# Fused attention and two expert layers on one core: the gate's clamp, log and sum in two column halves, and a start that is dealt out anew

## The chip, the cores and the metric

The kernel runs on one core of a Trainium2 chip, as one program. The metric is the device time of one launch in microseconds (us). Engines are named as in the profile: PE multiplies matrices, PEld is its weight load, DVE works on vectors, ACT evaluates functions, POOL is GpSimd, and SP issues the DMAs.

## The reference

Three blocks follow each other, all in float32. The kernel returns the last one.

```python
# attention with a decay: B, H, S, D = 4, 8, 576, 64
scores = (1/sqrt(D)) * q @ k.T
cum = cumsum(log(clip(f, 1e-4, 1.0)))          # one row of 576 gates for each of 32 heads
scores = where(causal, -1e9, scores + cum[:, None] - cum[None, :])
attn = softmax(scores) @ v                     # to x: 2304 tokens x 512
# first expert layer
x = ((x @ w1) * (x @ w2)) @ w3 @ w_out         # 512 -> 1024 -> 1024 -> 512
# second expert layer, on the normalized x
x = x / sqrt(mean(x*x) + 1e-6) * rms_g
out = silu(x @ w_gate) * (x @ w_val) @ w_out2  # 512 -> 1536 -> 512
```

## The kernel before

All work is listed as operations of a planner (`Plan`). Each has an engine, or a choice of engines, an estimated time, and the keys that it reads and writes. `Plan.order()` works out one order for each engine from these estimates and from due times, and the instructions are issued in that order. The keys serve the planner alone; the waits that the program really holds are put in by the framework, tile by tile. `TE` is the step between the due times of the first eight heads, `WC0` the due time of the first weight product.

**Heads.** Each of the 32 heads has 576 queries in five blocks. PE multiplies queries and keys into the PSUM tile `wide` (block 4) and into two banks (blocks 3 and 0, 2 and 1). DVE adds the mask and takes the row maximum (L439, tiles `PB0` to `PB4` and `nmax`; letters a and b for even and odd heads), ACT takes the exponential with the row sum (L447), PE transposes (L484), ACT and DVE copy the result (`PTf` for the first three heads, L500; `PTh` and `PTl` later), and PE multiplies it with the values into `wide` (L530 and L540). The tile `wide` serves scores and output in turn, so the next use waits until DVE has read it.

**Gates.** The decay comes in as additional rows of the factors: for the first two heads (`NQ`) rows 64 and on of `rq` and `rk` hold the cumulative sum, times 8 and times -8, beside constants. `start()` makes them. The gates of all heads are loaded in one DMA to `fc` (112 rows: the 32 heads twice, then heads 0 and 1 over the partitions that feed those rows), clamped on DVE (L1094), logged on ACT (L1095) and summed along the row by a scan on DVE (L1096) into `cum`. `first_rows` then writes the row block of `rq` on DVE (L1109) and of `rk` on ACT (L1111). The rows 64 to 127 of `rq` and `rk` were cleared before that on DVE (L1084). `cqx` takes the sums for the later heads (L1116, L1117, L260), which go to DRAM and come back head by head.

**Warming.** While PE has nothing to do it multiplies zeros (`zeros`, L1075): 7 products of 448 columns (`WARM`) at the start, and 4 more around the first head's scores. Nobody reads them.

**Weights.** The weights of the first layer arrive packed, and are unpacked (L572, L576 or L578, L582) and split into a high and a low part (L258 or L260, L251) on whichever of ACT, DVE and POOL the planner picks. 192 products (L656) of `w3` and `w_out` fill PE beside the first eight heads. When these heads are done `x_split` makes `xhl`, and the products of the first layer (L693, L718) follow, beside the rest of the heads. The second layer (L905, L986) comes when all heads are done.

Of the kernel before, what the change touches and what calls it, by code (L numbers as in the profile page):

```python
# [14 lines left out]
F32R = mybir.dt.float32r  # L15
U32 = mybir.dt.uint32
AF = mybir.ActivationFunctionType
# [5 lines left out]
P = 128  # L23
# [21 lines left out]
NR = 4  # L45
KH = KF2 // 2
FROWS = 112
WARM = 7
NQ, NP, QD = 2, 3, 6
WIDER = 3  # L50
NST = 3
# [1 line left out]

S0, TE, T1 = 0, 8200, 13400
LT, LP = 5000, 13000

WC0, WCP = 22000, 9000

FD, FR = 25000, 1.8

# [154 lines left out]
def body(ctx, tc, q, k, v, f, w12, w3, wo1, wgv, wo2, g, out):  # L217
# [13 lines left out]
    def t_dve(n, rate=1.04, lock=False):  # L231
        return "DVE", 70 + rate * n, lock

    def t_act(n, fixed=95):
        return "ACT", fixed + 0.833 * n, False
# [91 lines left out]
    cq = cqx[0:NH]  # L327
    cn = X[1].rearrange("p r n -> p (r n)")[0:NH, 0:2 * S].rearrange("p (r n) -> p r n", r=2)

    def load_f():  # L330
        SP.dma_start(out=fc, in_=f)

    def load_g():
        SP.dma_start(out=g_sb, in_=g)
# [107 lines left out]
    def row_exp(h, i, at):  # L442
        p, pr = h % 2, h // 2 % 2
        n, cols = QB[i][1], QEND[i]
        o = PB[p][i][:n, 0:cols]
        to = o if i else PB[p][4][0:n, 512:576]
        act(cols + 225, lambda: A.activation(to, o, AF.Exp, bias=nmax[p][:n, i:i + 1], scale=-1.0, accum_out=rsum[pr][:n, p, (i - 1) % 5:(i - 1) % 5 + 1]),  # L447
            [("nmax", p, i)] + ([] if i else [("PB", p, 4)]), [("PB", p, i), ("rsum", pr, p, i)], at)

    def attn_s(h, at):  # L450
        p = h % 2
# [1 line left out]
        t = t.rearrange("p (c n) -> p c n", c=2)  # L453
        QKh, w = QK, 1
        if h < NQ:
            QKh, w = [("rq", p), ("rk", p, 0), ("nrowq", p), ("nrown", p)], 2
        n1, n2 = st_next(h), st_next(h)
        o4 = [t[:, c, 0:288] for c in range(2)]
        o3, o0 = bank[n1][:, 0:448], bank[n1][0:64, 448:512]
# [14 lines left out]
    def transpose(h, parts, o, key, pt, at):  # L474
# [22 lines left out]
            for j in range(2):  # L497
                dma(147e3, lambda j=j: SP.dma_start(out=rall[j * D:(j + 1) * D, :], in_=r_o[j, 0:S].partition_broadcast(D)), [("rd", h // 2)], [("rall", j)])
        if h < NP:
            plan.op([t_act(n, 55), t_dve(n)], lambda e: (A.copy if e == "ACT" else V.tensor_copy)(PTf()[:, pt:pt + n], o[:, lo:lo + n]), [], [("PTf", pt), key] + ["fc", "one32", "cum"] * (h == 0))  # L500
            return
        act(n, lambda: A.copy(PTh[:, pt:pt + n], o[:, lo:lo + n]), [], [("PTh", pt), key], at, 55)  # L502
        m = n if pt != PT_KB3 else PT_Q0
# [571 lines left out]
        pe(896, lambda: T.matmul(bank[n][:, 0:448], mask[:, 0:P], mask[:, 0:448], start=True, stop=True), ["mask0", *r], [("bank", n)], at, 2)  # L1075

    def start():
        dma(157e3, load_f, w=["fc"], at=-100)
        load_qk(0, -90)
        dma(2e3, load_g, w=["g"], at=50000)  # L1080
        dve(300, lambda: V.memset(mask, 0.0), w=["mask", "mask0"])
        for p in range(2):

            dve(1030, lambda p=p: (V.memset(rq[p][D:P, :], 0.0), V.memset(rk[p][D:P, :], 0.0)), w=[("nrowq", p), ("nrown", p), ("rk", p, 1)])  # L1084

        for i in range(WARM):
            zeros(5, -1000)
        pool(580, make_ones, w=["one32", "cn1"], at=-50)
        pool(1100, make_masks, w=["ident", "mask", "ones"], at=-40)
        pool(2000, make_zeros, w=["zeros"], at=-30)  # L1090
        dve(70, lambda: V.memset(rows_c, 1.0), w=["picks"])
        dve(70, lambda: (V.memset(under, -0.501), V.memset(exp_in, 0.0)), w=["under", "exp"])
        act(1500, lambda: A.activation(rows_c[:, 0:1], rows_c[:, 0:1], AF.Ln), [], ["picks"])
        dve(300, lambda: V.tensor_scalar(out=fc, in0=fc, scalar1=1.0e-4, scalar2=1.0, op0=ALU.max, op1=ALU.min), ["fc"], ["fc"], -100)  # L1094
        act(S, lambda: A.activation(fc, fc, AF.Ln), ["fc"], ["fc"], -100)  # L1095
        dve(S + 650, lambda: V.tensor_tensor_scan(out=cum, data0=one32, data1=fc, initial=0.0, op0=ALU.mult, op1=ALU.add), ["fc", "one32"], ["cum"], -100)  # L1096
        hi, lo = cqx[:, 0, :], cqx[:, 1, :]

        def first_rows(h):
            r = slice(D + 32 * h, D + 32 * h + 4)  # L1100
            e = [ident[r, r.start + i:r.start + i + 1] for i in range(2)]
            c = rows_c[r, :]

            def picks():
                V.tensor_scalar_mul(c[:, 0:1], e[0], 8.0)
                V.tensor_scalar_mul(c[:, 1:2], e[1], -8.0)

            dve(100, picks, ["ident"], ["picks"])
            dve(480, lambda: V.tensor_scalar(out=rq[h][r, :], in0=cum[r], scalar1=c[:, 0:1], scalar2=e[1], op0=ALU.mult, op1=ALU.add),  # L1109
                ["cum", "ident", "picks"], [("nrowq", h)])  # L1110
            act(S, lambda: A.activation(rk[h][r, :], cum[r], AF.Identity, scale=c[:, 1:2], bias=e[0]),  # L1111
                ["cum", "ident", "picks"], [("nrown", h), ("rk", h, 1)], fixed=380)

        for h in range(NQ):
            first_rows(h)
        act(S, lambda: A.activation(hi.bitcast(F32R), cum, AF.Copy, scale=8.0), ["cum"], ["cq0"], -100)  # L1116
        dve(S, lambda: V.scalar_tensor_tensor(out=lo.bitcast(F32R), in0=cum, scalar=8.0, in1=hi, op0=ALU.mult, op1=ALU.subtract), ["cum", "cq0"], ["cq"], -100)  # L1117
        plan.op([("ACT", 1500, False)], lambda e: A.activation(exp_in, exp_in, AF.Exp), ["fc"], ["exp"], 0)
        copy(2 * S, cn, cq, ["cq", "cn1"], ["cn"], -1.0)
        prep(0, -90)  # L1120
        pool(1750, lambda: make_qk_rows(G), w=["rows", "Q2", "K2"])
        dma(150e3, lambda: SP.dma_start(out=cq_d, in_=cq), ["cq"], ["cdq"])
        dma(150e3, lambda: SP.dma_start(out=cn_d, in_=cn), ["cn"], ["cdn"])
        load_v(0, -70)
        prep_v(0, -60)
# [135 lines left out]
```

## Time and profile before

| what | value |
| --- | --- |
| median of 3 runs | 929.91 us (928.27 to 930.31) |
| the profiled execution | 930.35 us |
| its span in the trace | 928.5 us (1.85 us lie around it) |
| PE busy | 915.6 us, 99% of the span |
| PEld busy | 851.1 us, 92% |
| DVE busy | 802.9 us, 86% |
| ACT busy | 541.0 us, 58% |
| POOL busy | 144.4 us, 16% |
| granted TensorE clock | 1.00 |

Busy time is counted from an instruction's start to its end, and the instructions of an engine that overlap count once. The shares are means over a start, a stretch with heads, a stretch with heads and the first layer, and the second layer; the stretches are limited by different engines, so they are read stage by stage.

### The profile page before, as it was taken

Reading aid. Unit: us, or ns where it says so; the run is one execution under the profiler, and the core shown is the slowest. Engines: PE = TensorE matmul, PEld = TensorE weight load, DVE = VectorE, ACT = ScalarE, POOL = GpSimd, SP = SyncE. Lnnn points to the kernel's source line nnn. Section 1 sums busy time; section 2 is a strip of 40 time slices with the busy share of each in tenths; the row PEclk is TensorE's granted clock in tenths of the full one; section 3 lists DMA queues with packets and bytes.
Section 4 is the critical chain, followed back from the end, with each engine's and each line's share of the span. In section 5 each row is a group of like instructions: output and inputs, shape, how many; then the busy total and the mean of one; then the engine's idle time right before and its main releaser. Section 6 shows DMA issues by size and latency. Waiting matters only on the chain.

```text
span 928.5 us, 14596 instructions
## 1 busy us (share of the span) xinstructions
PE 915.6 (99%) x5111; PEld 851.1 (92%) x5111; DVE 802.9 (86%) x1518; ACT 541.0 (58%) x1101; POOL 144.4 (16%) x142
## 2 busy tenths in 40 slices
PE   8999999999999999999999999999999999999998
PEld 5678889899999999988899999999999999999998
DVE  8999999998989789846656789989988899888796
ACT  7899988776667776732322254555544465544452
POOL 1252222234203322030030310000000000000100
PEclk9999999999999999999999999999999999999999
DMA  7976595755766476428767236423743425633422
GB/s 234 298 241 200 165 309 190 260 197 170 254 209 206 143 251 204 154 98 314 253 202 299 97 109 215 169 103 113 273 170 120 142 69 171 203 119 122 134 68 102
DMA packets 49681, 170.69 MB, mean 184 GB/s; under 512 B 6129, under 2 KB 22048, under 8 KB 42440
## 3 DMA queue, kind: packets, MB, share of 16 engines
q1 hardware_dynamic: 49608, 169.77, 54.0%
q8 instruction: 40, 0.66, 0.3%
q14 instruction: 33, 0.27, 0.1%
HBM read 133.28 MB, written 32.63 MB: 179 GB/s over the span
## 4 chain that ended last, share of the span: by engine, by line
PE 86%; DVE 6%; issue 1%; DMA 0%; ACT 0%; DVEq 0%
PE bank L905 28%; PE bank L693 19%; PE bank L718 11%; PE bank L986 10%; PE wide L986 4%; PE bank L484 4%; PE wide L540 3%; PE bank L656 2%; PE bank L419 1%; PE bank L420 1%; DVE PTl L504 1%; DVE qk L251 1%; PE wide L420 1%; PE wide L419 1%; DVE wbig L251 1%
## 5 line engine op out<-in xcount | busy, mean ns | idle before, releaser
L693 PE MATMUL bank<-xhl,wbig 128*128 128x464 f32 (+1 forms) x960 | 215.5, 373 | 0.0
L693 PEld LDWEIGHTS bank<-xhl,wbig 128*128 128x128 f32 x960 | 176.6, 188 | 17.9
L905 PE MATMUL bank<-xop,wbig 128*128 128x384 f32 x1008 | 182.0, 334 | 0.0
L905 PEld LDWEIGHTS bank<-xop,wbig 128*128 128x128 f32 x1008 | 175.4, 188 | 0.2
L905 PE MATMUL bank<-xop,lbig 128*128 128x384 f32 x504 | 94.6, 334 | 0.0
L905 PEld LDWEIGHTS bank<-xop,lbig 128*128 128x128 f32 x504 | 88.0, 188 | 0.0
L504 DVE TENSOR_TENSOR PTl<-bank,PTh 128x512 fp32r<-128x512 f32 (+2 forms) x116 | 59.3, 531 | 4.4 <-ACT PTh L502 3.7
L502 ACT CAST PTh<-bank 128x512 fp32r<-128x512 f32 (+2 forms) x116 | 53.3, 488 | 15.5 <-PE bank L484 15.0
L718 PE MATMUL bank<-uh,Wch 128*128 128x464 f32 (+1 forms) x160 | 60.5, 378 | 0.0
L251 DVE TENSOR_TENSOR lbig<-zf,lbig 128x768 fp32r<-128x768 f32 x63 | 59.1, 949 | 0.6 <-ACT lbig L258 0.4
L718 PE MATMUL bank<-uh,Wcl 128*128 128x464 f32 (+1 forms) x160 | 59.3, 371 | 0.0
L718 PE MATMUL bank<-ul,Wch 128*128 128x464 f32 (+1 forms) x160 | 59.3, 371 | 0.0
L986 PE MATMUL bank<-lbig,wbig 128*128 128x384 f32 x324 | 57.9, 334 | 0.0
L986 PEld LDWEIGHTS bank<-lbig,wbig 128*128 128x128 f32 x324 | 56.3, 188 | 0.0
L258 ACT ACTIVATE lbig<-zf 128x768 fp32r<-128x768 f32 x39 | 33.0, 849 | 37.7 <-PE bank L986 12.8
L540 PE MATMUL wide<-PTh,V 128*128 128x512 f32 (+4 forms) x145 | 43.6, 312 | 1.3 <-DVE nmaxa L439 1.3
L911 DVE TENSOR_TENSOR zf<-cs 128x384 f32<-128x384 f32 x72 | 40.3, 559 | 5.1 <-ACT cs L916 3.2
L700 DVE TENSOR_TENSOR u<-bank,u 128x464 f32<-128x464 f32 (+1 forms) x40 | 25.3, 632 | 22.4 <-PE bank L693 22.3
L701 ACT CAST uh<-u 128x464 fp32r<-128x464 f32 (+1 forms) x40 | 23.1, 577 | 36.5 <-DVE u L700 36.3
L251 DVE TENSOR_TENSOR wbig<-nrm,wbig 128x768 fp32r<-128x768 f32 (+1 forms) x42 | 42.8, 1026 | 0.3
L927 ACT COPY cs<-bank 128x384 f32<-128x384 f32 x36 | 17.3, 481 | 41.1 <-PE bank L905 41.1
L698 ACT COPY u<-bank 128x464 f32<-128x464 f32 (+1 forms) x40 | 21.7, 542 | 29.3 <-PE bank L693 28.9
(265 smaller groups left out, 2083.7 us busy)
## 6 DMA issues: line engine op xcount, KB each, us to landing
xf<-sw_d SPq DMA_DIRECT2D x24, 896.0 KB
wbig<-w_d SPq DMA_DIRECT2D x12, 1024.0 KB
nrm<-sw_d SPq DMA_DIRECT2D x12, 896.0 KB
raw_w<-in_wgv SPq DMA_DIRECT2D x10, 1024.0 KB
sw_d<-raw_w SPq DMA_DIRECT2D x10, 896.0 KB
rk<-in_k SPq DMA_DIRECT2D x62, 144.0 KB
nrm<-wo_d SPq DMA_DIRECT2D x11, 768.0 KB
xf<-wo_d SPq DMA_DIRECT2D x10, 768.0 KB
```

The costliest lines, as they stand in the source:

```text
L251: plan.op([t_dve(n, lock=True), t_pool(n)], lambda e: on[e].tensor_sub(*(x() if callable(x) else x for x in (o, a, b_))), r, w)
L258: A.activation(o_, a_, AF.Copy, scale=by)
L484: T.transpose(o[:, c * P:(c + 1) * P], PB[p][i][:, kb * P:(kb + 1) * P], ident)
L502: act(n, lambda: A.copy(PTh[:, pt:pt + n], o[:, lo:lo + n]), [], [("PTh", pt), key], at, 55)
L504: dve(m, lambda: V.tensor_sub(PTl[:, pt:pt + m], o[:, lo:lo + m], f32(PTh[:, pt:pt + m])), [("PTh", pt)], [("PTl", pt), key], at)
L540: pe(w, lambda s_=s_, o=o, w=w, c=c, kb=kb, m=m, src=src: T.matmul(t[:, o:o + w], V2[p][:, kb, :], src[:, c:c + w], start=(s_ == 0 and m = ...
L693: T.matmul(o, a, x[:, kt, :], start=(kt == 0 and i == 0), stop=(kt == KD - 1 and i == 2))
L700: dve(w, lambda: V.tensor_mul(u, o, u), [("bank", n)], [("u", fb % 2)])
L718: T.matmul(o, a[:, es], x[:, ft, 0:w], start=(q == 0 and ft % 2 == 0 and i == 0), stop=(q == 3 and ft % 2 == 1 and i == 2))
L905: T.matmul(o, w[:, a, POS[j], kt], x[c][:, kt], start=start and kt == 0 and i == 0, stop=kt == 1 and i == 2, skip_group_check=not start)
L911: plan.op([t_dve(TH, lock=True), t_pool(TH)], lambda e: on[e].tensor_mul(o(), x(), y()), r, w)
L986: T.matmul(tiles[m], wv[:, a, k, m], z[c][:, kt], start=start and k == 0 and x == 0, stop=k == KH - 1 and x == 2, skip_group_check=not start)
```

## The change

The gates are loaded, clamped, logged and summed in two halves of 288 columns, and the second half is carried on from the last sum of the first by an addition to its first column. Rows 64 to 127 of the second head's `rq` and `rk` are cleared by POOL. `make_zeros` (zeros in the `PB` tiles) is listed after the sums, and the rows of `qk1` after the zeros. The load of the exponential's table is listed after the first head's rows in place of after the log. There are 5 warming products at the start in place of 7. `TE` goes from 8200 to 7800, `WC0` from 22000 to 20000.

```diff
-WARM = 7
+WARM = 5
...
-S0, TE, T1 = 0, 8200, 13400
+S0, TE, T1 = 0, 7800, 13400
...
-WC0, WCP = 22000, 9000
+WC0, WCP = 20000, 9000
...
-    def load_f():
-        SP.dma_start(out=fc, in_=f)
+    half = [slice(0, S // 2), slice(S // 2, S)]
+    CUM = [("cum", i) for i in range(2)]
+
+    def load_f(c):
+        SP.dma_start(out=fc[:, c], in_=f[:, c])
...
-        dma(157e3, load_f, w=["fc"], at=-100)
+        for i, c in enumerate(half):
+            dma(79e3, lambda c=c: load_f(c), w=[("fc", i)], at=-100)
...
-        for p in range(2):
-
-            dve(1030, lambda p=p: (V.memset(rq[p][D:P, :], 0.0), V.memset(rk[p][D:P, :], 0.0)), w=[("nrowq", p), ("nrown", p), ("rk", p, 1)])
+        def make_rows(e, p):
+            e.memset(rq[p][D:P, :], 0.0)
+            e.memset(rk[p][D:P, :], 0.0)
+
+        dve(1030, lambda: make_rows(V, 0), w=[("nrowq", 0), ("nrown", 0), ("rk", 0, 1)])
...
-        pool(2000, make_zeros, w=["zeros"], at=-30)
+        pool(1160, lambda: make_rows(G, 1), w=[("nrowq", 1), ("nrown", 1), ("rk", 1, 1)])
...
-        dve(300, lambda: V.tensor_scalar(out=fc, in0=fc, scalar1=1.0e-4, scalar2=1.0, op0=ALU.max, op1=ALU.min), ["fc"], ["fc"], -100)
-        act(S, lambda: A.activation(fc, fc, AF.Ln), ["fc"], ["fc"], -100)
-        dve(S + 650, lambda: V.tensor_tensor_scan(out=cum, data0=one32, data1=fc, initial=0.0, op0=ALU.mult, op1=ALU.add), ["fc", "one32"], ["cum"], -100)
+        for i, c in enumerate(half):
+            dve(150, lambda c=c: V.tensor_scalar(out=fc[:, c], in0=fc[:, c], scalar1=1.0e-4, scalar2=1.0, op0=ALU.max, op1=ALU.min), [], [("fc", i)], lock=True)
+            act(S // 2, lambda c=c: A.activation(fc[:, c], fc[:, c], AF.Ln), [], [("fc", i)], fixed=200)
+        for i, c in enumerate(half):
+            if i:
+                x, last = fc[:, c.start:c.start + 1], cum[:, c.start - 1:c.start]
+                dve(30, lambda: V.tensor_add(x, x, last), [CUM[0]], [("fc", 1)])
+            dve(S + 60, lambda c=c: V.tensor_tensor_scan(out=cum[:, c], data0=one32[:, c], data1=fc[:, c], initial=0.0, op0=ALU.mult, op1=ALU.add), [("fc", i), "one32"], [CUM[i]])
+        pool(650, make_zeros, [CUM[1]], ["zeros"])
...
-            act(S, lambda: A.activation(rk[h][r, :], cum[r], AF.Identity, scale=c[:, 1:2], bias=e[0]),
-                ["cum", "ident", "picks"], [("nrown", h), ("rk", h, 1)], fixed=380)
+            for i, n in enumerate(half):
+                act(S // 2, lambda n=n: A.activation(rk[h][r, n], cum[r, n], AF.Identity, scale=c[:, 1:2], bias=e[0]),
+                    [CUM[i], "ident", "picks", ("nrown", h), ("rk", h, 1)], [("nrown", h, i)], fixed=260)
...
-        plan.op([("ACT", 1500, False)], lambda e: A.activation(exp_in, exp_in, AF.Exp), ["fc"], ["exp"], 0)
+        plan.op([("ACT", 1500, False)], lambda e: A.activation(exp_in, exp_in, AF.Exp), [("nrown", 0, i) for i in range(2)], ["exp"], 0)
...
-        pool(1750, lambda: make_qk_rows(G), w=["rows", "Q2", "K2"])
+        pool(1750, lambda: make_qk_rows(G), ["zeros"], ["rows", "Q2", "K2"])
```

The planner's order moves with these lines, on every engine, up to the last head. Three places at the start show it; the names are those of the tiles, `tmp` holding `fc`, ones and `cum`.

On DVE, from the first clearing to the first row maximum, there stands before:

```order
L1084 MEMSET rk0_103 64x576
L1092 MEMSET tok_98 128x1 x2
L1084 MEMSET rq1_102 64x576
L1084 MEMSET rk1_104 64x576
L1105 TENSOR_SCALAR rows_c_130<-ident_95 4x1
L1106 TENSOR_SCALAR rows_c_130<-ident_95 4x1
L1094 TENSOR_SCALAR tmp_135<-tmp_135 112x576
L1096 SCALAR_TENSOR_TENSOR tmp_135<-tmp_135 112x576
L1109 TENSOR_SCALAR rq0_101<-tmp_135,rows_c_130,ident_95 4x576
...
L1117 SCALAR_TENSOR_TENSOR x0_131<-tmp_135,x0_131 112x576
L260 TENSOR_SCALAR x1_132<-x0_131 32x1152
L439 ISA PB4a_114,nmaxa_122<-wide_58,mask_129 128x576
```

and now, on the same engine and stretch:

```order
L1088 MEMSET rk0_103 64x576
L1098 MEMSET tok_98 128x1 x2
L1117 TENSOR_SCALAR rows_c_130<-ident_95 4x1
L1118 TENSOR_SCALAR rows_c_130<-ident_95 4x1
L1101 TENSOR_SCALAR tmp_135<-tmp_135 112x288 x2
L1107 SCALAR_TENSOR_TENSOR tmp_135<-tmp_135 112x288
L1106 TENSOR_TENSOR tmp_135<-tmp_135 112x1
L1107 SCALAR_TENSOR_TENSOR tmp_135<-tmp_135 112x288
L1121 TENSOR_SCALAR rq0_101<-tmp_135,rows_c_130,ident_95 4x576
...
L442 ISA PB4a_114,nmaxa_122<-wide_58,mask_129 128x576
```

The two clearings for head 1 are gone from ahead of the clamp, and the two operations for the later heads' sums (L1117 and L260 before) have moved from ahead of the first head's five row maxima to behind them.

On ACT, from the log to the second exponential of head 0, there stands before:

```order
L1095 ACTIVATE tmp_135<-tmp_135 112x576
L1118 ACT_TABLE_LOAD
L1118 ACTIVATE tok_98<-tok_98 128x1
L1111 ACTIVATE rk0_103<-tmp_135,ident_95,rows_c_130 4x576
L1116 ACTIVATE x0_131<-tmp_135 112x576
L1111 ACTIVATE rk1_104<-tmp_135,ident_95,rows_c_130 4x576
L572 ACTIVATE nrm_87<-nrm_87 128x1024
L447 ACTIVATE PB4a_114,rsuma_124<-PB4a_114,nmaxa_122 128x576
```

and now:

```order
L1102 ACTIVATE tmp_135<-tmp_135 112x288 x2
L1124 ACTIVATE rk0_103<-tmp_135,ident_95,rows_c_130 4x288 x2
L1131 ACT_TABLE_LOAD
L1131 ACTIVATE tok_98<-tok_98 128x1
L1124 ACTIVATE rk1_104<-tmp_135,ident_95,rows_c_130 4x288 x2
L1129 ACTIVATE x0_131<-tmp_135 112x576
L450 ACTIVATE PB4a_114,rsuma_124<-PB4a_114,nmaxa_122 128x576
```

The table load has moved from between the log and head 0's rows to behind these rows, and the first unpacking of a weight (`nrm`) from ahead of head 0's exponentials to behind all five.

On POOL, the clearings behind `ones` stand before as

```order
L340 MEMSET ones_96 128x128
L368 MEMSET qk1_107 64x576
L369 MEMSET qk1_107 4x576
L370 MEMSET qk1_107 64x576
L348 MEMSET PB1a_111 128x64
...
L350 MEMSET rsumb_125 128x10
```

and now as

```order
L343 MEMSET ones_96 128x128
L1087 MEMSET rq1_102 64x576
L1088 MEMSET rk1_104 64x576
L351 MEMSET PB1a_111 128x64
...
L353 MEMSET rsumb_125 128x10
L371 MEMSET qk1_107 64x576
L372 MEMSET qk1_107 4x576
L373 MEMSET qk1_107 64x576
```

POOL has two more clearings of 576 columns in this run of memsets, and the zeros hold no wait on DVE: the key of the sums orders them in the plan only, so they follow the clearings at once.

## Rows read from the trace of the kernel before

**Rows 1.** Windows: length, then busy us of PE, PEld, DVE, ACT, POOL; clock, DMA.
```profile
0.00:20.00 20.00, 17.84 (x60) 10.10 (x60) 16.17 (x40) 14.34 (x27) 3.98 (x20) 1.00 0.77 255
20.00:40.00 20.00, 18.54 (x95) 12.81 (x96) 18.46 (x45) 15.61 (x38) 5.80 (x4) 1.00 0.85 257
40.00:100.00 60.00, 55.94 (x319) 45.93 (x318) 59.18 (x124) 57.11 (x126) 20.29 (x19) 1.00 0.74 231
100.00:120.00 20.00, 20.00 (x111) 16.92 (x111) 19.11 (x42) 17.61 (x38) 6.17 (x5) 1.00 0.45 129
120.00:180.00 60.00, 58.12 (x335) 52.01 (x334) 59.01 (x120) 47.30 (x106) 17.39 (x14) 1.00 0.77 263
180.00:920.00 740.00, 740.00 (x4170) 708.46 (x4169) 630.75 (x1152) 388.05 (x768) 90.81 (x80) 1.00 0.50 172
```

**Rows 2.** Timeline of PE: start, us, what, xcount [idle before <-releaser].
```profile
1.52 7.05 PE L1075 MATMUL bank<-mask 128*128 128x448 f32 x14 [1.52 <-DVE rows_c L1091]
8.47 1.24 PE L417 MATMUL wide<-rk,rq 128*128 128x288 f32 x4
...
15.83 0.27 PE L484 MATMUL bank<-ident,PB1a 128*128 128x128 f32 x1
...
17.36 1.14 PE L417 MATMUL wide<-rk,rq 128*128 128x288 f32 x4
...
20.22 3.16 PE L530 MATMUL wide<-PTf,rv 128*128 128x512 f32 x10 [0.86 <-ACT raw_x L572]
```

**Rows 3.** Timeline of PEld, the last two weight loads of the first warming run.
```profile
7.27 0.19 PEld L1075 LDWEIGHTS bank<-mask 128*128 128x128 f32 x1 [0.19 <-issue]
7.65 0.19 PEld L1075 LDWEIGHTS bank<-mask 128*128 128x128 f32 x1 [0.19 <-issue]
```

**Rows 4.** Timeline of DVE from the clearing of head 1's rows on.
```profile
3.08 0.54 DVE L1084 MEMSET rq<- 64x576 f32 x1 [0.16 <-issue]
...
4.48 0.82 DVE L1094 TENSOR_SCALAR tmp<-tmp 112x576 f32<-112x576 f32 x1
6.05 1.36 DVE L1096 TENSOR_TENSOR_SCAN tmp<-tmp 112x576 f32<-112x576 f32 x1 [0.75 <-ACT tmp L1095]
...
9.16 0.76 DVE L1117 SCALAR_TENSOR_TENSOR x<-tmp,x 112x576 fp32r<-112x576 f32 x1 [0.35 <-ACT x L1116]
9.95 0.75 DVE L260 TENSOR_SCALAR x<-x 32x1152 f32<-32x1152 f32 x1
10.63 0.74 DVE L439 CUSTOM_DVE_ANT_0 PB4a<-wide,mask 128x576 f32<-128x576 f32 x1
...
17.03 1.21 DVE L582 SCALAR_TENSOR_TENSOR raw_ul<-raw_ul 128x1024 uint32<-128x1024 uint32 x1
18.16 0.68 DVE L260 TENSOR_SCALAR w<-nrm 128x1024 fp32r<-128x1024 f32 x1
...
19.37 0.74 DVE L439 CUSTOM_DVE_ANT_0 PB4b<-wide,mask 128x576 f32<-128x576 f32 x1
```

**Rows 5.** Timeline of ACT: log, table, head 0's rows, first exponential.
```profile
5.33 0.68 ACT L1095 ACTIVATE tmp<-tmp 112x576 f32<-112x576 f32 x1 [3.11 <-DVE tmp L1094]
6.04 1.28 ACT L1118 ACT_TABLE_LOAD   x1
...
7.56 0.86 ACT L1111 ACTIVATE rk<-tmp,ident,rows_c 4x576 f32<-4x576 f32 x1
...
12.62 0.77 ACT L447 ACTIVATE PB4a<-PB4a,nmaxa 128x576 f32<-128x576 f32 x1
```

**Rows 6.** Timeline of POOL, a clearing and the last memset of its first run.
```profile
3.70 0.57 POOL L370 MEMSET qk<- 64x576 f32 x1
...
4.89 0.10 POOL L350 MEMSET rsumb<- 128x10 f32 x1
```

**Rows 7.** Groups by form, DVE, 0 to 125 us: busy us, mean ns | idle.
```profile
L260 DVE TENSOR_SCALAR w<-raw_x 128x1024 fp32r<-128x1024 f32 x1 | 1.9, 1921 | 0.0
```

**Rows 8.** Groups by form, ACT, 0 to 125 us.
```profile
L576 ACT ACTIVATE raw_ul<-raw_ul,tok 128x1024 uint32<-128x1024 uint32 x2 | 2.5, 1240 | 0.0
```

## What the change will do: a prediction

> **What bounds the kernel now.** I read three views in this order. First the windows [rows 1]: from 180 to 920 us PE is busy 740.00 of 740 us, so nothing later than 180 us can be gained but by beginning it earlier. Before 180 us PE is free for 2.16, 1.46, 4.06, 0 and 1.88 us in the five stretches, 9.56 in all. From 40 to 100 us DVE is busy 59.18 of 60 us and ACT 57.11, so there the two engines set the pace and PE fills in. POOL is far from full everywhere. The granted clock is 1.00 throughout.
>
> Second, the two orders of PE. Ahead of the first product of the first expert layer (L693) stand the same instructions in both, but for two warming products: all 192 weight products, 144 transposes, the scores and outputs of the first heads. The useful PE work is thus the same before and behind that point. The time changes by what the start takes, and by how much PE waits before about 180 us.
>
> Third, the timelines of the start. PE multiplies zeros from 1.52 us on and begins the first useful product at 8.47 [rows 2]. The chain ahead of it is the clamp at 4.48 (0.82 us), the log at 5.33 (0.68), the scan at 6.05 (1.36) and head 0's rows of `rk` at 7.56 (0.86), which end at 8.42 [rows 4, 5]. The exponential's table loads beside the scan and is off the chain: it begins at 6.04 and takes 1.28, and the scan ends at 7.41. From there to the output product of head 0 at 20.22 the one gap that PE shows is 0.86 us ahead of it [rows 2]. The releaser named there, a weight unpacking on ACT, has nothing to do with these products. They write `wide`, in which head 1's scores (17.36 to 18.50) lie until DVE has taken their row maximum, and DVE takes that at 19.37 to 20.11 since it is on weight work until then [rows 2, 4].
>
> **The change part by part.** *Clearing of head 1's rows.* DVE loses two memsets of 0.54 us that begin at 3.08 [rows 4]. With their gaps they take 1.1 us, and all of it lies ahead of the clamp, so the clamp may begin at 3.38 in place of 4.48, if its gates have landed. When they land the trace does not show, only that it is by 4.48. So the clamp's start lies between 3.38 and 4.48; I take 3.9, the middle.
>
> *Halves.* For a half I take these durations: clamp 0.41 (half of 0.82, the dear end), log 0.43 and rows 0.61 (0.68 and 0.86 less 0.25; half of the log's 0.68 would be 0.34, and some of it is fixed), scan 0.70 (half of 1.36 and a little). The addition of one column is a new instruction; its nearest row is an operation with two inputs of 576 columns (L1117, 0.76 [rows 4]), so it lies between nothing and 0.76, and for one column I take 0.15. The path is clamp, log, scan, addition, scan, rows of `rk`: 0.41 + 0.43 + 0.70 + 0.15 + 0.70 + 0.61 = 3.00, with 0.35 for six hand-overs (0.03 to 0.15 each before) 3.35. Before it took from 4.48 to 8.47, 3.99. The second half's clamp and log lie beside the first half's log and scan. The halves thus give 0.64 us, and with the clamp at 3.9 the first score product may begin at 7.25. Bounds: 6.73 and 7.83.
>
> *Warming.* Two products are four passes, and the passes follow each other at 0.38 us, from 7.27 to 7.65 [rows 3]. With two of these steps behind the last load the run ends at about 8.4, so without four passes PE is free at about 6.9 and does not hold up the product at 7.25; it idles for 0.35 us. With seven it would be in the way until 8.4. Bounds for the first product: 6.9 and 7.83, a gain of 0.64 to 1.57; I take **1.2**.
>
> *The later heads' sums.* L1117 and L260 (0.76 + 0.75 us) stood on DVE between the first scores and the first row maximum at 10.63 [rows 4]. They now stand behind five row maxima. What waits for them is the DMA of the sums to DRAM, behind which stand on SP only loads for heads 2 and 3; head 2's scores come behind head 0's output, which ends at 23.4 [rows 2]. I cost this at nothing, up to 1 us if those loads become late.
>
> *Table load.* It is no longer beside the scan but behind head 0's rows, and costs ACT 1.28 us ahead of head 1's rows (four halves at 0.61 for two of 0.86 in all) and of the first exponential. With head 0's rows done at 7.2, the load, the dummy exponential (0.2), head 1's rows (1.22) and the 0.68 for `cqx` put the first exponential at 10.6. Before it stood at 12.62, behind a weight unpacking that waited for its DMA [rows 5]. That unpacking now stands behind the five exponentials. So the load costs nothing; if the exponentials were due at once it would cost 1.5 us.
>
> *The gap ahead of head 0's output.* The transposes began at 15.83 [rows 2], 7.36 us after the first product, PE being busy all between. So they come at about 14.6. On DVE, four weight operations stood ahead of head 1's last row maximum; now one combining step (1.21 us) and one cast (0.68) fewer stand ahead of it [rows 4]. DVE then reaches it at about 17.0, and the scores are there at 15.83 - 1.2 + (18.50 - 15.83), 17.3. So the output begins at about 18.2 and the 0.86 us gap is gone but for a rest: **0.8**.
>
> *Due times and order.* These move work between engines over the first 32 heads. Ahead of the first `x_split` subtraction I counted both orders and priced each instruction by its group's mean. DVE has at the start about 1.1 us less, and beyond it 8 instructions fewer and 9 more of 0.27 to 1.21 us, 0.6 more in all. ACT has 0.9 more at the start and 2.3 more beyond, mostly two bit steps of 1.24 [rows 8]. POOL has 3.5 more. ACT had 15.3 us free before 120 us, 10 of them before 40, so I let its 3.2 us go into these: nothing, with bounds of 3.0 gained (DVE's work ahead of the fifteenth head's row maximum is 3.0 less) and 3.2 lost.
>
> *Sum.* 1.2 + 0.8 = 2.0 us of 930.35 (span 928.5 and 1.85 around it) make 928.35. The median of the runs lies 0.44 lower than this execution, so I predict **927.9**.
>
> One rule speaks against the change. The clamp took 0.82 us, against 0.68 for a DVE cast of 1024 columns, nearly twice as many, and POOL ran memsets until 4.99, to within 0.3 us of its end [rows 4, 6]; another DVE cast of 1024 columns took 1.92 [rows 7]. So DVE operations of this kind seem to be held while POOL works. POOL's run of memsets is now longer by two of 0.57 and ends at about 6.1, so both clamps lie in it. The Trainium skill, page "SBUF — State Buffer", section "SBUF: two separate sides", says the same: DVE in a two-port mode and GpSimd take one shared pair of ports for a whole instruction, and the other one blocks.
>
> **The rivals.**
> - *The clamps are held.* Each half waits for a memset of up to 0.57 us. With the gates late too (clamp at 4.48), the first product begins at 7.83 and some 0.4 later, 8.2. The start then gives 0.3 in place of 1.2: 928.8. Against it: with the gates early PE's own 6.9 hides most of it.
> - *DVE gives nothing on.* From 40 to 100 us DVE is 99% busy [rows 1], and ahead of the first layer it has only 0.5 us less work. If PE's lead of 2 us is lost while it waits for DVE there, 0.5 remain: 929.4. Against it: the 1.54 us that DVE idles from 20 to 40 us can be used if head 0 and 1 are earlier.
> - *The new order gives more.* Heads due earlier and more splits on POOL: 3.0 us by the fifteenth head, 926.9.
> - *ACT becomes the bound, and it is slower.* ACT is 95% busy from 40 to 100 us [rows 1] and gets 3.2 us more work ahead of the first layer. If its free time before 40 us can't take that, since the exponentials and unpackings there wait for other engines, the layer begins 3.2 later less the 1.2 of the start: 931.9. It decides once ACT finds room for less than 1.2 of the 3.2 us.
>
> That the change does nothing is no rival: the two clearings and the warming passes are gone in the order.
>
> **How the numbers follow.** Chances: the forecast 0.47, the clamps held 0.10, DVE gives nothing on 0.20, more 0.13, ACT the bound 0.10. A difference under 0.2% (1.86 us) can't be told from no change here. The forecast lies at the edge of this; with its start between 0.64 and 1.57 and some of the order's gain in reach I give it two thirds beyond the edge. Faster: 0.31 + 0.13 and a little of the others, 0.46. Slower: 0.10. Same: 0.44. The range reaches from 925.8 (more, with a good start) to 930.6 (all given back and 0.7 lost in the order); the forecast's own is 927.0 to 928.8.
>
> **What would show it.** The first L417 product (now L420) at 7 to 7.8 us; both clamps ahead of 5 us; the first exponential at about 10.6; the output of head 0 at about 18.2 with no gap ahead; PE free for about 7.5 of the first 180 us in place of 9.56; the first L693 product about 2 us earlier than before. It is wrong if the first exponential waits for ACT beyond 12, if PE's free time from 40 to 100 us grows by what the start gave, or if ACT is busy for nearly all of that stretch.

## The result and the profile after

| what | before | after |
| --- | --- | --- |
| median, measured side by side | 928.82 us (927.92 to 933.05, 14 runs) | 934.71 us (931.42 to 937.15, 14 runs) |
| ratio | 1 | 1.0059, 95% interval 1.0045 to 1.0073 |
| profiled execution, span | 930.35, 928.5 | 937.15, 935.4 |

The change makes the kernel slower by 0.6%. I had predicted 927.9 us, a gain. (One of the 14 runs, at 1508.7 us with a clock of 0.557, was disturbed; it is left out of the range and the ratio, and without it the median is 934.13.) The profiled execution took the longest of the other 13, so the views below add up to more than the median's loss.

The windows of after answer [rows 1] (length, then busy us of PE, PEld, DVE, ACT, POOL, then the clock and DMA). The last stretch ends at 920 us in both.

```profile
0.00:20.00 20.00, 18.45 (x58) 10.31 (x58) 15.64 (x44) 15.32 (x32) 5.15 (x22) 1.00 0.77 256
20.00:40.00 20.00, 18.21 (x87) 12.96 (x87) 16.75 (x37) 15.50 (x34) 2.74 (x2) 0.83 0.82 261
40.00:100.00 60.00, 56.58 (x316) 45.60 (x315) 58.82 (x127) 59.10 (x130) 21.15 (x20) 1.00 0.69 226
100.00:120.00 20.00, 18.53 (x101) 15.20 (x101) 18.13 (x39) 14.57 (x32) 3.51 (x4) 1.00 0.41 125
120.00:180.00 60.00, 55.25 (x317) 48.97 (x316) 58.95 (x111) 46.73 (x101) 18.17 (x14) 1.00 0.72 239
180.00:920.00 740.00, 740.00 (x4170) 707.75 (x4169) 626.56 (x1148) 391.63 (x777) 99.64 (x89) 1.00 0.52 174
```

From 180 us on PE is still busy without a break. Before that it is free for 1.55, 1.79, 3.42, 1.47 and 4.75 us, 12.98 in all, where it was 9.56 before: 3.42 more. The stretch from 40 to 100 us, where ACT is now busy 59.10 of 60 us, has even become better (3.42 free in place of 4.06). The loss lies in the last two stretches before 180 us, and in the clock, which reads 0.83 from 20 to 40 us. The windows around that place (same columns):

```profile
27.00:28.00 1.00, 0.19 (x1) 0.22 (x2) 1.00 (x6) 1.00 (x4) 0.57 (x1) 0.83 0.87 166
28.00:34.00 6.00, 6.00 (x11) 2.97 (x12) 4.78 (x7) 4.43 (x11) 0.00 (x0) 0.50 0.99 348
34.00:35.00 1.00, 1.00 (x6) 0.82 (x6) 0.00 (x0) 0.00 (x0) 0.00 (x0) 0.75 0.94 349
```

For some 6.5 us PE works at 1.2 GHz, half its speed, and loses 3.0 + 0.25 = 3.25 us while it counts as busy. The sum: 3.42 of idle time, 3.25 of clock, less 0.23 because the first warming run is shorter (6.82 us in place of 7.05), is 6.4 of the 6.9 us by which the span grew. Where the other half microsecond went the views don't show.

The timeline of PE (start, us, what, count, [idle before <-releaser]) answers [rows 2]:

```profile
1.51 6.82 PE L1078 MATMUL bank<-mask 128*128 128x448 f32 x10 [1.51 <-DVE rows_c L1097]
8.17 1.13 PE L420 MATMUL wide<-rk,rq 128*128 128x288 f32 x4
...
19.00 2.84 PE L533 MATMUL wide<-PTf,rv 128*128 128x512 f32 x8
...
27.81 5.30 PE L533 MATMUL wide<-PTf,rv 128*128 128x512 f32 x8 [1.66 <-ACT PTf L503]
...
128.32 0.47 PE L543 MATMUL wide<-PTh,V 128*128 128x512 f32 x1 [3.37 <-DVE nmaxa L442]
```

The same two places before:

```profile
27.42 3.17 PE L530 MATMUL wide<-PTf,rv 128*128 128x512 f32 x10 [0.38 <-DVE nmaxa L439]
...
122.66 0.47 PE L540 MATMUL wide<-PTh,V 128*128 128x512 f32 x1 [1.32 <-DVE nmaxa L439]
```

Head 0's output comes 1.2 us earlier than before (19.00 for 20.22). Head 1's output at 27.81 is already 0.4 later than before (27.42), behind 1.66 us of waiting in place of 0.38, and here the half clock begins: its products take 5.30 us, as many of head 0 took 2.84. Head 9's output at 128.32 waits 3.37 us; before it stood at 122.66 behind 1.32.

Both waits are for `wide`, and both end with a row maximum on DVE, though the releaser named at 27.81 is a copy on ACT. DVE at the first of them, from head 1's block 4 (`PB4b`) to head 2's (`PB4a`), after:

```profile
18.13 0.76 DVE L442 CUSTOM_DVE_ANT_0 PB4b<-wide,mask 128x576 f32<-128x576 f32 x1 [0.36 <-PE wide L420]
...
22.79 0.75 DVE L539 COPY x<-wide 64x576 f32<-64x576 f32 x1 [0.27 <-PE wide L536]
23.46 1.21 DVE L585 SCALAR_TENSOR_TENSOR raw_ul<-raw_ul 128x1024 uint32<-128x1024 uint32 x1
...
25.48 1.56 DVE L251 TENSOR_TENSOR w<-nrm,w 128x1024 fp32r<-128x1024 f32 x1
26.96 0.74 DVE L442 CUSTOM_DVE_ANT_0 PB4a<-wide,mask 128x576 f32<-128x576 f32 x1
```

and before, where the first of these two maxima stands at 19.37 [rows 4]:

```profile
23.84 0.63 DVE L578 TENSOR_SCALAR raw_x<-raw_x 128x1024 uint32<-128x1024 uint32 x1
...
25.38 1.21 DVE L251 TENSOR_TENSOR w<-nrm,w 128x1024 fp32r<-128x1024 f32 x1
26.52 0.74 DVE L439 CUSTOM_DVE_ANT_0 PB4a<-wide,mask 128x576 f32<-128x576 f32 x1
```

The weight subtraction directly ahead of the maximum is no new one: it stood there before, at 1.21 us, and takes 1.56 now. New in this stretch are the copy of head 0's output, which ACT made before, and a combining step of 1.21 us where a bit step of 0.63 stood. So from one maximum to the next DVE now takes 8.83 us, where it took 7.15. PE was 1.2 us earlier at head 0's output and is 0.4 later at head 1's.

And DVE ahead of the second, after and before:

```profile
119.33 1.21 DVE L251 TENSOR_TENSOR wbig<-raw_x,wbig 128x1024 fp32r<-128x1024 f32 x1
120.47 0.68 DVE L663 TENSOR_TENSOR Wcl<-bank,Wch 128x512 fp32r<-128x512 f32 x1
121.07 1.21 DVE L585 SCALAR_TENSOR_TENSOR raw_ul<-raw_ul 128x1024 uint32<-128x1024 uint32 x1
...
122.74 1.80 DVE L251 TENSOR_TENSOR xhl<-x,xhl 128x928 fp32r<-128x928 f32 x1
...
125.54 1.83 DVE L251 TENSOR_TENSOR xhl<-x,xhl 128x928 fp32r<-128x928 f32 x1
127.41 0.76 DVE L442 CUSTOM_DVE_ANT_0 PB4a<-wide,mask 128x576 f32<-128x576 f32 x1
```
```profile
115.62 1.73 DVE L582 SCALAR_TENSOR_TENSOR raw_ul<-raw_ul 128x1024 uint32<-128x1024 uint32 x1
...
117.96 1.64 DVE L251 TENSOR_TENSOR xhl<-x,xhl 128x928 fp32r<-128x928 f32 x1
...
120.72 1.11 DVE L251 TENSOR_TENSOR xhl<-x,xhl 128x928 fp32r<-128x928 f32 x1
121.76 0.74 DVE L439 CUSTOM_DVE_ANT_0 PB4a<-wide,mask 128x576 f32<-128x576 f32 x1
```

At the second wait the new order puts two more weight operations (`wbig<-raw_x`, `Wcl`) between head 10's small row maxima and the large one, and its second subtraction of `xhl` takes 1.83 us where it took 1.11. The longer subtractions fit POOL's work. After:

```profile
24.82 1.13 POOL L260 TENSOR_SCALAR wbig<-raw_ul 128x1024 fp32r<-128x1024 f32 x1 [18.61 <-DVE raw_ul L585]
...
122.43 1.14 POOL L260 TENSOR_SCALAR wbig<-raw_ul 128x1024 fp32r<-128x1024 f32 x1 [6.33 <-PE bank L659]
124.98 1.41 POOL L251 TENSOR_TENSOR qk<-rq,qk 64x576 fp32r<-64x576 f32 x1 [1.42 <-PE bank L659]
```

The first still runs for 0.47 us when DVE begins the subtraction at 25.48, the other two for 0.83 and 0.85 us when it begins those of `xhl`. Before, the 1.64 us one began at 117.96 while POOL worked from 117.49 to 118.63, and the 1.11 us one met none.

Last, the start, on DVE and ACT [rows 4, 5], and PE's weight loads [rows 3]:

```profile
3.17 1.38 DVE L1101 TENSOR_SCALAR tmp<-tmp 112x288 f32<-112x288 f32 x2
4.47 0.74 DVE L1107 TENSOR_TENSOR_SCAN tmp<-tmp 112x288 f32<-112x288 f32 x1
5.31 0.16 DVE L1106 TENSOR_TENSOR tmp<-tmp 112x1 f32<-112x1 f32 x1
5.51 0.76 DVE L1107 TENSOR_TENSOR_SCAN tmp<-tmp 112x288 f32<-112x288 f32 x1
```
```profile
6.30 0.62 ACT L1124 ACTIVATE rk<-tmp,ident,rows_c 4x288 f32<-4x288 f32 x1 [0.37 <-DVE tmp L1107]
6.93 1.28 ACT L1131 ACT_TABLE_LOAD   x1
...
10.21 0.78 ACT L450 ACTIVATE PB4a<-PB4a,nmaxa 128x576 f32<-128x576 f32 x1
```
```profile
6.16 0.34 PEld L1078 LDWEIGHTS bank<-mask 128*128 128x128 f32 x1 [0.41 <-issue]
6.90 0.33 PEld L1078 LDWEIGHTS bank<-mask 128*128 128x128 f32 x1 [0.41 <-issue]
7.42 0.19 PEld L1078 LDWEIGHTS bank<-mask 128*128 128x128 f32 x1 [0.19 <-issue]
```

Head 0's rows are ready at 6.92, earlier than the 7.2 I forecast. But the warming products step at 0.75 us until 6.90, and the weight load at 7.42 is the first that takes 0.19 us in place of 0.33, so PE is not free before 8.17. In the profile of before the step of 0.75 us ended at 4.64. The kernel with the old due times below has the same warming products and shows the change of pace at 4.66:

```profile
3.91 0.34 PEld L1078 LDWEIGHTS bank<-mask 128*128 128x128 f32 x1 [0.41 <-issue]
4.66 0.21 PEld L1078 LDWEIGHTS bank<-mask 128*128 128x128 f32 x1 [0.41 <-issue]
5.06 0.19 PEld L1078 LDWEIGHTS bank<-mask 128*128 128x128 f32 x1 [0.19 <-issue]
```

So the pace of the first microseconds is a matter of the execution and not of the kernel. The clock column doesn't show it: it reads 1.00 from 0 to 20 us in both profiles.

### The profile page after: what moved, and what is told of

The parts are those of the page before. It is cut to its first block, busy times and chain, and to the rows that moved or that the text cites. A ratio compares the mean times of both kernels' runs of the same rounds, so it can differ in the third digit from the quotient of the medians.

```text
span 935.4 us, 14602 instructions
## 1 busy us (share of the span) xinstructions
PE 918.9 (98%) x5107; PEld 852.4 (91%) x5107; DVE 801.9 (86%) x1513; ACT 545.0 (58%) x1103; POOL 150.4 (16%) x151
## 4 chain that ended last, share of the span: by engine, by line
PE 86%; DVE 8%; ACT 3%; issue 2%; DMA 0%; SPq 0%; DVEq 0%; ACTq 0%
PE bank L908 28%; PE bank L696 18%; PE bank L721 11%; PE bank L989 10%; PE wide L989 4%; PE bank L487 4%; PE wide L543 3%; PE bank L659 1%; DVE PTl L507 1%; PE bank L423 1%; PE bank L422 1%; PE bank L1078 1%; PE wide L533 1%; DVE qk L251 1%; DVE wbig L251 1%
## 5 line engine op out<-in xcount | busy, mean ns | idle before, releaser
L507 DVE TENSOR_TENSOR PTl<-bank,PTh 128x512 fp32r<-128x512 f32 (+3 forms) x116 | 59.4, 531 | 2.8 <-ACT PTh L505 2.3
L543 PE MATMUL wide<-PTh,V 128*128 128x512 f32 (+4 forms) x145 | 43.4, 311 | 3.4 <-DVE nmaxa L442 3.4
```

The lines of the kernel that those rows point to most:

```text
L507: dve(m, lambda: V.tensor_sub(PTl[:, pt:pt + m], o[:, lo:lo + m], f32(PTh[:, pt:pt + m])), [("PTh", pt)], [("PTl", pt), key], at)
L543: pe(w, lambda s_=s_, o=o, w=w, c=c, kb=kb, m=m, src=src: T.matmul(t[:, o:o + w], V2[p][:, kb, :], src[:, c:c + w], start=(s_ == 0 and m = ...
```

## The experiments

Each run was timed beside the kernel before; a ratio is to it. Kernels marked (table) issue the operations in an order written out as a list in place of the planner's; all else is the code of before or after, and their lines in the profile are some 70 later (L615 is L543).

**The start and the order apart (both table).** The operations of `start()` as in after and every later operation in the order and on the engine that it had before; and the reverse.

```diff
-        for i, e, _ in plan.order():
+        for i, e in ORDER:  # after's start, before's order behind it / before's start, after's order behind it
             plan.ops[i][1](e)
```

> The changed start (halves, second head's rows on GpSimd, table load behind head 0's rows, 5 warming products), and behind it the instructions of all later work on each engine in the order of the kernel before. Theory A (the new order behind the start costs the time): 928 to 929 us, PE's clock 1.00 in all runs. Theory B (the start itself does, since PE is warmed less and reaches the waits for DVE earlier): 933 to 935 us, with stretches at half clock between 20 and 40 us.

Measured: 928.23 us (927.46 to 929.92), ratio 0.9988 (0.9979 to 0.9998).

> The start of the kernel before, and behind it the later work in the order of the changed kernel. Theory A: 933 to 935 us. Theory B: 928.5 to 930 us and a clock of 1.00 throughout.

Measured: 936.54 us (934.71 to 937.28), ratio 1.0074 (1.0059 to 1.0089), a little above theory A's 933 to 935, with the same wait of 3.37 us ahead of head 9's output. The start gains about 1.1 us (0.0012 of 929.4) and the order of what follows costs about 6.9 (0.0074 of it). That settles that the loss comes from the order behind the start, of all engines together.

**One gap at a time (table).** Two products of zeros on PE in the wait at 26 us; and the weight subtraction behind the row maximum there, on DVE.

```diff
 L487 MATMUL bank<-ident,PB4b 128x128
+L1078 MATMUL bank<-mask 128x448 x2
 L533 MATMUL wide<-PTf,rv 128x512
```
```diff
-L251 TENSOR_TENSOR w<-nrm,w 128x1024
 L442 ISA PB4a,nmaxa<-wide,mask 128x576
+L251 TENSOR_TENSOR w<-nrm,w 128x1024
```

> The changed kernel, with two more products of zeros on PE (four passes, about 1.5 us) in the gap of 1.66 us ahead of head 1's output; nobody reads them. Theory C (the gap lets the clock fall to 1.2 GHz for about 7 us, which costs some 3.4 us): clock 1.00 in all runs and 931 to 932 us, like the two undropped runs of the changed kernel (931.42 and 932.16). If the clock has nothing to do with the gap: 934 to 937 us as before.

Measured: 933.44 us (932.92 to 933.96), ratio 1.0043 (1.0028 to 1.0058).

> The changed kernel with one instruction moved on DVE: the low part of the weight w (1.56 us from 25.48 us on) comes behind the row maximum of head 2's block 4 in place of ahead of it. Theory C: the maximum is taken 1.5 us earlier, the gap on PE shrinks from 1.66 to under 0.6 us, the clock stays at 1.00 and the time is 930.5 to 932 us. If the copies on ACT hold the output: the gap stays above 1.2 us and the time at 934 to 937.

Measured: 934.37 us (932.53 to 936.78), ratio 1.0060 (1.0042 to 1.0079). Neither run reached the time that theory C named for it. In both the clock holds at 26 us, and in both profiles it now falls behind the wait at 125 us (0.91 from 120 to 140 us). Closing one gap left the other to do the same. With one gap closed this could not be told from the loss having another cause.

**Both row maxima earlier (table).** As the last, and on DVE the second subtraction of `xhl` and the weight combining `raw_ul` behind head 10's row maximum, with POOL's copy that needs the latter.

```diff
-L585 SCALAR_TENSOR_TENSOR raw_ul<-raw_ul 128x1024
-L251 TENSOR_TENSOR xhl<-x,xhl 128x2x464
 L442 ISA PB4a,nmaxa<-wide,mask 128x576
+L251 TENSOR_TENSOR xhl<-x,xhl 128x2x464
+L585 SCALAR_TENSOR_TENSOR raw_ul<-raw_ul 128x1024
```

> The changed kernel with two of DVE's row maxima earlier: head 2's block 4 ahead of the weight subtraction (as in the run max_first), and head 10's block 4 ahead of the second subtraction of xhl and of a weight combining. Theory 'two gaps and the clock behind them': the 3.4 us gap at 125 us shrinks to under 0.8, the clock stays at 1.00, and the time falls by the gap's 3 us and by 2 to 4 us of half clock: 928 to 930. Rival 'a gap comes back elsewhere' (as when the first gap alone was closed: 934.4): PE waits for xhl or for the delayed weight by about as much, or another of its gaps of 1 to 2 us lets the clock drop: 932 to 934.5.

Measured: 932.49 us (931.38 to 935.23), ratio 1.0038 (1.0024 to 1.0052). The wait for the row maximum is gone, and a few products later PE waits for a weight:

```profile
118.88 0.47 PE L616 MATMUL wide<-PTh,V 128*128 128x512 f32 x1 [0.61 <-ACT qk L331]
...
123.30 2.95 PE L769 MATMUL bank<-xhl,wbig 128*128 128x464 f32 x8 [1.73 <-DVE wbig L324]
```

Behind these 1.73 us the clock fell again. 932.49 is the rival's number: the gap moved.

**Which number deals the bad order.** The changed kernel with the due times back, both and one at a time.

```diff
-S0, TE, T1 = 0, 7800, 13400
+S0, TE, T1 = 0, 8200, 13400    # due_back, wc_only
-WC0, WCP = 20000, 9000
+WC0, WCP = 22000, 9000         # due_back, te_only
```

> The changed kernel with TE back at 8200 and WC0 back at 22000, so that the planner deals out the rest from the new start alone. If the due times make the bad order: 928 to 929, as with the new start and the old order (928.23). If the planner deals a worse order from any other start, since the start's estimates move with it: 931 or more, with a gap of over 2 us somewhere before 180 us.

Measured: 928.41 us (927.63 to 928.95), ratio 0.9989 (0.9979 to 0.9998).

> The changed kernel with WC0 back at 22000 (TE stays 7800). If TE alone makes the gaps: 933 to 936. If WC0 makes them: 928 to 930. If each order is its own draw of the planner: in between, with gaps at other places than 27 and 125 us.

Measured (TE 7800, WC0 22000): 930.23 us (927.57 to 931.85), ratio 1.0008 (0.9998 to 1.0018).

> The changed kernel with TE back at 8200 (WC0 stays 20000). If WC0 alone makes the gaps: 933 to 936. If TE makes them: 928 to 930. If each order is its own draw of the planner: in between, with gaps at other places than 27 and 125 us.

Measured (TE 8200, WC0 20000): 934.40 us (932.61 to 935.63), ratio 1.0055 (1.0039 to 1.0072). So moving `WC0` to 20000 costs the time; `TE` alone costs about 1.8 us over `due_back`. The gaps of `wc_only` stand elsewhere, though, the longest 2.25 us at 32.57, again with half the clock behind it. That wait ends with an exponential on ACT, so it is not one row maximum that `WC0` delays.

**WC0 the other way.** `WC0` 24000, `TE` 8200.

```diff
-WC0, WCP = 20000, 9000
+WC0, WCP = 24000, 9000
```

> The new start with TE at 8200 and WC0 moved the other way, to 24000. If the loss follows WC0's direction (weight work taken too early keeps DVE from the row maxima): 927.5 to 929, no gap of over 1.5 us. If each order is a draw of its own: 930 to 935, with gaps of over 1.5 us at places that nothing in the number foretells.

Measured: 933.40 us (933.0 to 934.68), ratio 1.0049 (1.0036 to 1.0063). The other direction costs nearly as much. Its profile shows no low clock, but 10.88 us of free PE before 180 us (2.64 of them in one gap at 38.66), 1.6 more than `due_back`'s, and 0.4 behind 180 us. The warming run takes 0.9 us more (6.51 in place of 5.59). Of the 4.7 us between the two profiled executions that leaves 1.7 which I could not place. The direction of `WC0` explains nothing here: of three values both outer ones lose, which fits an order that is drawn anew for each value. Three values can't show more.

**A late row maximum in the good order (table).** The kernel of 928.23 with one wait made longer.

```diff
-L442 ISA PB4a,nmaxa<-wide,mask 128x576
 L510 TENSOR_TENSOR PTh<-bank,PTh 64x128
 L663 TENSOR_TENSOR Wcl<-bank,Wch 128x512
 L251 TENSOR_TENSOR wbig<-nrm,wbig 128x1024
+L442 ISA PB4a,nmaxa<-wide,mask 128x576
```

> The new start with the old order (928.23), and one thing made worse: DVE takes the row maximum of head 10's block 4 behind a copy of Wcl and a weight subtraction instead of ahead of them. PE, ACT, POOL and SP keep their order. Theory 'gaps and the clock behind them': PE's wait ahead of head 9's output grows from 1.32 to about 3.4 us, like the changed kernel's; the time is 2 us more in executions where the clock holds and up to 3.5 us more again where it falls: 930.3 to 933.8, with a wider spread than 927.5 to 929.9. Rival 'PE makes it up, DVE's total work is what counts' (DVE does the same work in another order): 928 to 929.

Measured: 931.06 us (930.61 to 932.74), ratio 1.0024 (1.0015 to 1.0033). PE's wait and the windows around it:

```profile
122.15 0.47 PE L615 MATMUL wide<-PTh,V 128*128 128x512 f32 x1 [3.55 <-DVE nmaxa L514]
```
```profile
122.00:126.00 4.00, 3.85 (x15) 3.65 (x16) 1.51 (x3) 2.25 (x6) 0.74 (x2) 0.57 1.02 350
126.00:128.00 2.00, 2.00 (x11) 1.77 (x11) 1.39 (x3) 1.97 (x4) 0.78 (x1) 1.00 1.06 259
```

The gap is 2.2 us longer, and the time 2.8. DVE does the same work in all, and PE makes up only a part: the clock of 0.57 from 122 to 126 us costs 1.7 more, and of these 3.9 us 3.1 are left at the end (from the start of the wait, 118.60 in this profile and 120.87 in that of `start_new_order_old`, to the ends of the spans, 928.9 and 928.1). The single operation that stands late is enough.

**The clock alone (table).** Zeros on PE in both waits of the changed kernel; nothing waits less for it.

```diff
+    for n in [5] * 2 + [3] * 8:    # bridge_both; [3] * 4 in bridge_4
+        zeros(n, 0)
```

> The changed kernel with products of zeros in both long gaps: 2 ahead of head 1's output (as in the run bridge) and 8 ahead of head 9's output, some 3 us. They only fill waiting. Theory 'half of the loss is the clock': the gap at 125 us is left under 0.8 us, the clock is 1.00 in every stretch, and the time is 3 us or so under the changed kernel's: 930.5 to 932.5. Rival 'the clock costs nothing' (the low readings are only a mark of idle time): 934 to 935.5.

Measured: 934.24 us (933.57 to 934.42), ratio 1.0055 (1.0042 to 1.0067), the clock 1.00 in every stretch. That is the rival's number, but no test of it, for I had sized the products wrongly: one has two passes of 0.38 us, so 8 take 6 us, and ran on for 2.6 us beyond a wait of 3.4. Head 9's output came 21.56 us after head 8's, where with the gap left open (`bridge`) it was 19.45.

> The changed kernel with 2 products of zeros ahead of head 1's output and 4 (3.0 us) ahead of head 9's output, in place of the 8 that took 6 us. The waits stay as long as they are. Theory 'half of the loss is the clock': clock 1.00 throughout, no gap over 0.8 us left at these two places, and 2.3 us less than with 8: 931.5 to 932.3, which is 2.4 to 3.2 under the changed kernel. Rival 'the clock costs nothing': 934 to 935.

Measured: 931.45 us (930.93 to 932.45), ratio 1.0020 (1.0011 to 1.0029).

```profile
122.17 0.47 PE L616 MATMUL wide<-PTh,V 128*128 128x512 f32 x1 [0.38 <-DVE nmaxa L515]
```

Six products that nobody reads lower the ratio from 1.0059 to 1.0020, 3.6 us (by the medians, 2.7 from 934.13), and narrow the spread from 5.7 us to 1.5. Two executions of the changed kernel kept the clock of themselves (1.000) and took 931.42 and 932.16 us. So the half clock behind the gaps makes up half to two thirds of the loss, and most of the spread; the rest is the waiting.

**The start's warming, with the old due times.** 4 and 3 products in place of 5.

```diff
-WARM = 5
+WARM = 4    # warm4; 3 in warm3
```

> The new start with TE 8200 and WC0 22000 (928.41) and 4 warming products in place of 5. In executions in which PE stays at its slow pace until 7.4 us the first score product begins at 7.5 instead of 8.2, in those in which it speeds up at 4.6 it begins at 6.95 as before, behind a gap of 0.8 us. Theory 'warming at half pace is in the way': median 0.2 to 0.5 us lower, 927.9 to 928.2. Rival 'the gap keeps the clock from rising, or lets it fall': 929 to 931.

Measured: 927.95 us (927.65 to 928.17), ratio 0.9986 (0.9977 to 0.9994).

> The new start with TE 8200 and WC0 22000 and 3 warming products in place of 5 or 4 (928.41, 927.95). Theory 'warming at half pace is in the way': the six passes end by 6.2 us even at half pace, the first score product begins at 6.95 in every execution, behind a gap of 0.7 us or more, 927.8 to 928.0. Rival 'the gap keeps the engine at half pace longer': the first scores and transposes run at half pace, 928.3 to 930.

Measured: 928.14 us (927.58 to 930.61), ratio 0.9985 (0.9975 to 0.9995). In the profile of `warm4` the first score product begins at 6.96 and head 0's output at 17.86. Three products gain nothing over four, and the spread grows again. `warm4` has the lowest median of the study, though its ratio can't be told from those of `due_back` and `warm3`.

**A shorter wait in the good order (table).** In `warm4`, head 10's row maximum ahead of the second subtraction of `xhl`.

```diff
-L251 TENSOR_TENSOR xhl<-x,xhl 128x2x464
 L442 ISA PB4a,nmaxa<-wide,mask 128x576
 L510 TENSOR_TENSOR PTh<-bank,PTh 64x128
+L251 TENSOR_TENSOR xhl<-x,xhl 128x2x464
```

> The kernel of 927.95 (new start, TE 8200, WC0 22000, 4 warming products) with DVE's second subtraction of xhl (1.11 us) behind head 10's row maximum of block 4 and one small subtraction instead of ahead of it. PE, ACT, POOL and SP keep their order. Theory 'PE's gaps before 180 us add to the end one for one': the 1.32 us gap ahead of head 9's output shrinks by 1.1, and the time is 1.0 to 1.1 less, 926.9. Rival 'DVE makes it up elsewhere': the products of xhl begin as late as before, 927.8 to 928.1.

Measured: 928.18 us (927.79 to 929.42), ratio 0.9986 (0.9977 to 0.9994): the rival's number to within 0.1. PE waits 1.0 us less ahead of the output, and then for the weight that DVE brings that much later:

```profile
119.84 0.47 PE L615 MATMUL wide<-PTh,V 128*128 128x512 f32 x1 [0.28 <-DVE nmaxa L514]
...
123.43 3.63 PE L768 MATMUL bank<-xhl,wbig 128*128 128x464 f32 x16 [0.90 <-DVE wbig L323]
```

An operation put late cost most of its delay (`late_max`); one put early gave nothing where DVE was the next to be waited for.

## Why the prediction was wrong

**The step that failed is "Due times and order".** I priced the moved work by engine totals and cost it at nothing, since DVE had 0.5 us less in all ahead of the first layer and ACT had free time. The totals were the wrong quantity. By the two split runs the order costs about 6.9 us, beyond both my bounds for it (3.0 gained, 3.2 lost). What decides is how much work the producing engine has between its earlier results and the one that PE waits for: 8.83 us of DVE from head 1's last maximum to head 2's where it was 7.15, and 3.1 us of weight work at 119.33 where 1.7 stood before. `late_max` shows the rule on one operation; which waits make up the whole 6.9 us no run shows, since each wait that I closed came back elsewhere. I had compared the orders at three places of the start and, beyond it, only counted.

**What I had no rival for is the clock.** All windows of before read 1.00 [rows 1], and I took that as given. Behind the gap of 1.32 us that before had ahead of head 9's output it held; behind the new order's gaps PE fell to 1.2 GHz for 3 to 7 us. `bridge_4` shows that this is half of the loss or more.

**The rival "ACT becomes the bound"** gave 931.9 and the right sign, but by the wrong mechanism. ACT is busy 59.10 of 60 us from 40 to 100 us, as I named for a sign of it, and PE is free less in that stretch than before. **"DVE gives nothing on"** named the right engine, and took from the forecast only 1.5 us for it; `warm4_max` and `both_first` show its mechanism at work. Of the signs that I named for a success, PE is free for 12.98 us before 180 us in place of the 7.5 forecast, and the first product of the first layer begins at 130.32, 5.65 later than before and not 2 earlier.

**The start was right in mechanism and near in size.** The clamps began at 3.17 (I took 3.9) and the two took 1.38 us (I took 0.41 each): held beside POOL's memsets, it seems, as the rival said, but early enough. Scans 0.74 and 0.76 (0.70), addition 0.16 (0.15), rows 0.62 (0.61), first exponential 10.21 (10.6). Where the pace rises early the first product begins at 6.97 (`due_back`; 7.25 forecast) and head 0's output at 17.88 (18.2 forecast). In the profiled execution of after the pace rose late, the first product stood at 8.17, and head 0's output at 19.00. *Warming* was the mis-sized term: I took its end at 6.9 from one execution, and the first product behind five warming products came at 6.96 (`start_new_order_old`) to 8.26 (`te_only`). The later heads' sums and the table load cost nothing that shows, as forecast. The start alone came to 1.1 us by `start_new_order_old`, against the 1.2 of my sum. The 0.8 us for the gap ahead of head 0's output hang on the later order: in that run's profile PE still waits 1.14 us there. In `due_back` the gap is gone, as forecast, but waits of 0.82 and 0.76 us stand behind it, at 22.44 and 26.01, and the whole gain is 1.0 us in place of 2.0.

**The range** of 925.8 to 930.6 fits the start without the due times (928.23, 928.41, 927.95); for the change as it stands it was 4 us too low.

What stays open: why one gap is followed by half clock and another of its length is not (below), 1.7 and 1.9 us of the loss of `wc_later` and `wc_only` against `due_back` that neither idle PE nor the clock nor the pace of the start shows, and how much of the planner's order could be foreseen.

## What to carry to other kernels

Where a planner's numbers are touched, read the new order at each place at which the bounding engine waits for a result, and price what now stands ahead of it on the producing engine; here totals per engine didn't tell. Change the work and the planner's numbers in separate steps: here the work gained 1.1 us and a due time moved by 2 us cost some 6 (`wc_only` against `due_back`), and the same due time moved the other way cost nearly as much. A gap on PE may cost more than its length, so bridge one that can't be closed, with no more products than fit.

## What the runs showed of the hardware

- **Half clock behind a gap depends on more than the gap's length.** It followed gaps of 1.66 us (after, at 27.81), 1.73 (`both_first`, 123.30), 2.25 (`wc_only`, 32.57) and 3.55 (`late_max`, 122.15). It did not follow gaps of 1.66 (`start_new_order_old`, 16.11), 1.75 (after, 42.45), 2.64 (`wc_later`, 38.66) or the 3.37 of after at 128.32, while the very same wait of 3.37 us in `start_old_order_new` was followed by it (0.83 from 120 to 140 us).
- **The first products' pace changes at another time in each execution:** with products of the same kind from 1.51 us on, at 4.6 us in before, 5.2 in `bridge_4`, 6.7 in `late_max` and 7.4 in after. Between `bridge_4` and after, which have one order up to there, head 0's output moved with it from 17.89 to 19.00.
- **DVE subtractions are held while POOL works.** Those of `xhl` took 1.11 us alone and 1.64, 1.80 and 1.83 beside a POOL operation that still ran for 0.67 to 0.85 us; that of `w` took 1.21 alone and 1.56 beside one that ran for 0.47 more. The Trainium skill, page "SBUF — State Buffer", section "SBUF: two separate sides", says that a DVE operation with two SBUF inputs and a GpSimd operation that reads SBUF exclude each other for a whole instruction; the trace agrees to within 0.15 us, since 1.11 + 0.85 would be 1.96 where 1.83 was measured.
